# Four weight conversions on ScalarE, each tied behind a copy that TensorE waits for

## The chip, the cores and the metric

The kernel runs on one core of one Trainium2 chip. The metric is the device time of one execution in microseconds (us). TensorE (PE) multiplies, ScalarE (ACT) and VectorE (DVE) copy and do elementwise work, GpSimd (POOL) helps with transposes, and SyncE (SP) issues most transfers.

## The reference, cut to what matters

```python
# q, k, v: (8 batches, 8 heads, 576 tokens, 64), float32
kv = einsum('bhsd,bhse->bhde', k, v)
out = einsum('bhsd,bhde->bhse', q, kv)
rms = sqrt(mean(out * out, axis=-1, keepdims=True) + 1e-06)
x = (out / rms * g_norm)            # then laid out as (4608 tokens, 512)

a = x @ w1                          # w1, w2: 512 x 1024
b = x @ w2
h = a * b @ w3                      # (a * b) @ w3, w3: 1024 x 1024
return h @ w_out                    # w_out: 1024 x 512, result float32
```

The weights w1, w2, w3 and w_out arrive as 64-bit floats, and the kernel turns them into 32-bit floats itself. w3 and w_out are multiplied with each other once ("folded"), so that each group of tokens needs only `(a * b) @ (w3 @ w_out)`. g_norm is multiplied into w1 and w2.

## The kernel before

The tokens are worked on in nine groups of 512. Before the first group there are two halves of eight steps in which w3 and w_out are folded. Each step turns a chunk of w3 on PE, copies the turned chunk from PSUM with ScalarE, and multiplies. Batch 0 of the attention and the conversion of weights run beside it. A conversion handles 128 x 1024 values, in two halves: `begin_next` does two operations on ScalarE, `end_next` four on VectorE and, for w1 and w2, the scaling by g.

```python
def conversion(n, dst, raw, cols=slice(0, 1024), scale=None, by_scalar=False):
    ...
    low = ab[n % 2][:, NF // 2:]...                      # one of two buffers
    nc.scalar.activation(low, lo, AF.Copy, scale=2.0 ** -51, bias=2.0)      # line 157
    nc.scalar.activation(dst, hi.bitcast(FP32), AF.Abs)                     # line 158
    yield                                                # here begin_next ends
    nc.vector.scalar_tensor_tensor(out=low_bits, in0=hi, ...)               # line 160
    nc.vector.tensor_scalar(out=dst, ..., op0=ALU.max, op1=ALU.min)         # line 164
    nc.vector.tensor_scalar(out=dst_bits, ..., op0=ALU.logical_shift_left)  # line 167
    nc.vector.tensor_tensor(out=dst_bits, in0=dst_bits, in1=low_bits, op=ALU.add)   # line 170
    if scale is not None:
        scale_by(dst, scale, by_scalar)   # line 133 on ScalarE in the first group, else line 135 on VectorE

def turn_w3(half, c):
    ...four transposes on PE (line 583)...
    nc.scalar.copy(w3T[half, c], t_ps)                                      # line 588

def fold_chunk(half, c, ms):
    for m in ms:
        nc.tensor.matmul(sums_ps[half][m], lhsT=w3T[half, c][:, m, :], ...) # line 596
        if c == KF - 1:
            nc.scalar.copy(w3o_sb[:, half * NH + m, :], sums_ps[half][m])   # line 601

def turn(r):                                             # x, normed, turned for the products
    ...four transposes on PE (line 449)...
    nc.scalar.copy(dst, t_ps.rearrange("p (i j) t -> p i (j t)", i=2))      # line 451
```

The products with w1 and w2 are done in four blocks p = 0 to 3, each with seven products of half the size in place of eight. PE works on one product (8 matmuls) while ScalarE copies the last one out of PSUM. Copies and products stand in this order; `r1` and `r2` are PSUM banks that are written again, so each copy has to be done before the next product in its bank begins:

```python
def winograd(lhsT, rhs, chunks, done, between=lambda: None):
    ...
    def keep(name, ps):
        ...
        nc.scalar.copy(t, ps)                                               # line 630
    r1 = product("a11", "b11")                                              # line 617, all products
    p1 = keep("p1", r1)
    r2 = product("s1", "t1")
    p5 = keep("p5", r2)
    product("s2", "t2", r1)
    u2 = keep("u2", r1)
    between()                                            # attention of the next batch, in p = 1 to 3
    product("s4", "b22", r2)
    done("c12", r2, u2)
    product("s3", "t3", r1)
    u3 = keep("u3", r1)
    done("c22", p5, u3)
    r3 = product("a12", "b21")
    done("c11", r3, p1)
    between()
    product("a22", "t4", r1)
    done("c21", r1, None)
```

`done` adds and multiplies on VectorE (lines 756, 757, 753) or copies on ScalarE (line 752). The sums s1 to s4 of the weights (lines 670, 671) and the differences t1 to t4 of x (line 660) are made by VectorE. `between` brings in kv products (line 332, copied by line 343), turned q (line 351, copied by line 353) and q times kv (line 415).

The main loop for the first group, T == 0:

```python
for p in range(NF):
    ...
    gates(T, p, between if T or p else lambda: None)     # the seven products of block p
    if T == 0:
        if p + 1 < NF:
            run(sum_w(p + 1))
        for _ in range(2):
            if len(converted) < len(todo):
                begin_next()
                end_next()
```

Four conversions are left for this loop: two at p = 0 (the two halves of the weights for block 2) and two at p = 1 (those for block 3). The order of instructions on PE, GpSimd and SyncE is as written. In this part of the kernel, that on ScalarE and VectorE is chosen by a scheduler when the program is built; it does not know when a transfer lands.

Of the kernel before, what the change touches and what calls it, by code (L numbers as in the profile page):

```python
# [21 lines left out]
def kernel(  # L22
# [32 lines left out]
    nc = tc.nc  # L55
# [26 lines left out]
    def bank(pool, tag):  # L82
        return pool.tile([P, 512], FP32, name=tag, tag=tag)


    loaded = {}
    q_left = {}

    kv_left = [const.tile([P, H, D], FP32, name=f"{name}l_sb") for name in "kv"]
# [129 lines left out]
    def conversions(n):  # L219

        what, i = todo[n]
        if what == "w":
            dst = w_sb[:, i].rearrange("p w c f -> p (w c f)")

            return [conversion(n, dst, raws[n], scale=g_col, by_scalar=in_first_group)]
        if what == "b":
            return [conversion(n, chunks[:, 2 * i:2 * i + 2, 0, :], raws[n])]
        dst = chunks[:, i].rearrange("p w f -> p (w f)")
        cuts = [[0, 256, 512, 1024], [0, 512, 1024], [0, 1024]][min(i, 2)]
        return [conversion(n, dst, raws[n], slice(a, b)) for a, b in zip(cuts, cuts[1:])]  # L230
# [4 lines left out]
    def begin_next():  # L235
        if len(begun) < len(todo):
            begun.append(conversions(len(begun)))
            for c in begun[-1]:
                next(c)
# [25 lines left out]
    xT = {B: x_left}  # L265
# [48 lines left out]
    def attention(b):  # L314
# [129 lines left out]
        def turn(r):  # L444

            t_ps = bank(ps_at, "at").rearrange("p (j t) -> p j t", j=J)
            m = 2 * (r % 2)
            for j in range(J):
                nc.tensor.transpose(t_ps[:, j, :], st[r // 2][:, j // 2, j % 2, m:m + 2, :], ident)  # L449
            dst = xT[b][:, r // 2, :, r % 2, :]  # L450
            nc.scalar.copy(dst, t_ps.rearrange("p (i j) t -> p i (j t)", i=2))

        def x_by_dma(h):

# [63 lines left out]
    def steps(b):  # L518

        a = batch(b)
        a.start()
        more = b + 1 < B
        fs, ends = ([[] for _ in range(8)] for _ in range(2))

        def turn(i, f, *args, next_group=False):

            t = []  # L530

            def begin():
                t.append(f(*args))
                next(t[0])
                next(t[0])

            fs[i].append((begin,))
            (to_end if next_group else ends[i + 1]).append((lambda: all_of(t[0]),))

        if to_end:  # L540

            ends[0] += [(lambda: nc.gpsimd.tensor_copy(tick, late["p5"][:, 0, 0:1]),), *to_end]
        to_end.clear()
        odd = b % 2
        if b == 1:
            fs[0] += [(a.begin_kv, 0, 1), (a.begin_q, 0, 1)]
        fs[1] += [(a.begin_kv, 2, 3), (a.finish, 0)]
        if b == 1:
            fs[2] += [(a.q_t_left,), (a.begin_q, 2, 3)]
            fs[3] += [(a.turn, 0), (a.turn, 1)]  # L550
        else:
            turn(1, a.q_two_by_dma, 2, 3)
            turn(2, a.x_by_dma, 0)
            if odd:
                turn(1, a.q_left_by_dma)
        second = 5 if b == 1 else 4
        if more:
            fs[second].append((batch(b + 1).begin_kv, 0, 1))
        fs[second].append((a.finish, 1))
        if odd:  # L560
            fs[second].append((a.product_left,))
        if b == 1:
            turn(6, a.x_by_dma, 1)
            turn(7, a.x_left_by_dma, next_group=True)
        else:
            turn(5, a.x_by_dma, 1)
            if odd:
                turn(5, a.x_left_by_dma, next_group=more)
        if more:
            turn(7 if b == 1 else 5, batch(b + 1).q_two_by_dma, 0, 1, next_group=True)  # L570
            fs[7 if odd else 0].append((load_q_left, b + 1))
        return iter([lambda s=e + f: [f(*args) for f, *args in s] for e, f in zip(ends, fs)])
# [34 lines left out]
    def late_tile(name):  # L607
        return late_pool.tile([P, 7, P], FP32, name=name[0] if name[0] == "u" else name)

    def winograd(lhsT, rhs, chunks, done, between=lambda: None):  # L610


        def product(a_name, b_name, to=None):
            ps = to if to is not None else bank(ps_mm, "mm").rearrange("p (u n) -> p u n", u=2)
            for u in range(2):
                for c in range(chunks):
                    nc.tensor.matmul(  # L617
                        ps[:, u, :],
                        lhsT=lhsT(a_name, u, c),
                        rhs=rhs(b_name, c),  # L620

                        start=(u == 0 and c == 0 and to is None),
                        stop=(c == chunks - 1),
                        skip_group_check=True,
                    )
            return ps

        def keep(name, ps):
            t = late_tile(name)[:, 0:4, :].rearrange("p (u a) n -> p u (a n)", u=2)
            nc.scalar.copy(t, ps)  # L630
            late[name] = t
            return t

        r1 = product("a11", "b11")
# [16 lines that stand above are left out]
# [78 lines left out]
    def sum_ab(p):  # L729
        aa[p] = {f"a{i + 1}{j + 1}": ab[j][:, p, i, :] for i in range(2) for j in range(2)}  # L730
        return sums(aa[p], free["ab", p])
# [94 lines left out]
    def load_b():  # L826
        n = len(loaded_b)
        if n == ALL_B:
            return
        t = streams[n % len(streams)]  # L830

        part = {ALL_B - 2: 6, ALL_B - 1: 7}.get(n, n % 7)

        queue = nc.scalar if n % 7 in (3, 5) else nc.sync
        if n + 1 < ALL_B:
            queue.dma_start(out=t, in_=w3o_l2[part])
        else:
            t = t[:, 0:1024]
            queue.dma_start(out=t, in_=w3o_l2[part, :, 0:1024])
        loaded_b.append(t)  # L840
# [260 lines left out]
    for n, T in enumerate(groups):  # L1101
        pieces = steps(T + 1) if n + 2 < NG else iter([])

        def between():
            next(pieces, lambda: None)()
            if T == 1:
                for _ in range(2):
                    if next(preparing, 0) == 0 and len(loaded_b) < 3:
                        load_b()

        for p in range(NF):
            if T and p + 1 == NF:
                sum_1, sum_2, sum_4, sum_3 = sum_ab(p)
                following = {
                    "c12": [], "c22": [sum_1],
                    "c11": [
                        lambda: sum_inner(0, lambda: all_of(f() for f in (sum_2, sum_3))),
                        lambda: sum_inner(1),
                    ],
                    "c21": [sum_4],  # L1120
                }

                in_order = tc.manual_schedule(engines={mybir.EngineType.DVE})
                in_order.__enter__()
                gates(T, p, between, lambda name: all_of(f() for f in following[name]))
                continue
            gates(T, p, between if T or p else lambda: None)
            if T == 0:
                if p + 1 < NF:
                    run(sum_w(p + 1))  # L1130
                for _ in range(2):
                    if len(converted) < len(todo):
                        begin_next()
                        end_next()
                if p + 1 == NF:
                    allocate_projection()
                    run(*(f(i) for i in range(NF) for f in (sum_ab, combine_w3o)))
            else:
                run(sum_ab(p))
        last = n + 1 == NG  # L1140
        if T:
            project_twice(T, last, [] if last else combine_x(groups[n + 1]))
            in_order.__exit__(None, None, None)
            continue
        project(T, between)
        run(combine_x(1))
        preparing = prepare_b()
        third = late_pool.tile([P, 3, 2, P], FP32, name="inner_sums")
        inner_sums.append([third[:, i] for i in range(3)])
# [30 lines left out]
```

## Time and profile before

| | |
|---|---|
| time, three runs | 768.45, 769.53, 770.31 us |
| span of the profiled run | 769.8 us |
| busy ScalarE | 252.7 us, 33% |
| busy VectorE | 543.7 us, 71% |
| granted TensorE clock | 1.000 |

The page of a profile gives shares of engines and a chain of waits, followed back from the last instruction. A timeline lists instructions with their start, length, engine, line, operation and tiles, and in brackets the idle time of that engine just before, with what ended it. PEld is TensorE's loading of weights, which overlaps with its matmuls. "w_sb" are the converted w1 and w2, "raw" the 64-bit weights as loaded, "ab" buffers that hold turned w3 or halves of conversions before they hold a * b, "mm" and "at" banks of PSUM, "ws" sums of weights, "xc" and "xT" the x of a group.

### The profile page before, as it was taken

How to read it: one execution, taken by the hardware profiler on the slowest of the kernel's cores; microseconds unless marked ns; L12 is line 12 of the kernel's file. 1: busy time of each engine (PE TensorE's matmuls, PEld its weight loads, DVE VectorE, ACT ScalarE, POOL GpSimd, SP SyncE). 2: the span in 40 equal slices, each digit the busy share in tenths (PEclk: the TensorE clock that was granted, in tenths of full speed). 3: DMA queues.
4: the chain of work that ended last, by engine and by line, in shares of the span. 5: the costliest groups of instructions: out<-in, count | busy, mean ns of one | idle time of the engine just before them, and what ended most of it. 6: DMA issues, size and time to landing. Idle time of an engine off the chain costs nothing.

```text
span 769.8 us, 14414 instructions
## 1 busy us (share of the span) xinstructions
PE 760.1 (99%) x5775; PEld 661.2 (86%) x5775; DVE 543.7 (71%) x1083; ACT 252.7 (33%) x479; POOL 136.2 (18%) x132
## 2 busy tenths in 40 slices
PE   8999999999999999999999999999999999999998
PEld 6455688888899889988998899889988998898897
DVE  7978999548978568856775687557755864495467
ACT  6777744313322332233222321232133222222221
POOL 0000000123520442043114411331144000000000
PEclk9999999999999999999999999999999999999999
DMA  9997532329997834874487448734842370064015
GB/s 324 324 333 213 186 120 60 84 69 267 323 296 265 235 101 115 275 215 102 122 269 206 116 138 267 200 103 132 284 83 50 139 251 1 1 239 152 1 32 195
DMA packets 133159, 132.55 MB, mean 172 GB/s; under 512 B 76644, under 2 KB 121188, under 8 KB 133092
## 3 DMA queue, kind: packets, MB, share of 16 engines
q1 hardware_dynamic: 130640, 116.81, 51.3%
q10 hardware_dynamic: 2452, 14.81, 5.5%
q8 instruction: 46, 0.75, 0.4%
q14 instruction: 21, 0.17, 0.1%
HBM read 100.27 MB, written 16.38 MB: 152 GB/s over the span
## 4 chain that ended last, share of the span: by engine, by line
PE 92%; DMA 5%; SPq 1%; ACT 1%; issue 0%; DVE 0%; ACTq 0%
PE mm L617 60%; PE mm L894 20%; PE mm L596 6%; PE at L332 3%; PE at L415 2%; DMA raw<-w3o_l 2%; DMA raw<-in_moe_w_dram 1%; DMA raw<-in_moe_w_out_dram 1%; DMA w3o_sb<-w3o_l 1%; PE at L583 1%; SPq L95 0%; PE at L945 0%; PE at L351 0%; ACT ab L157 0%; PE at L449 0%
## 5 line engine op out<-in xcount | busy, mean ns | idle before, releaser
L617 PE MATMUL mm<-xT,w_sb 128*128 128x256 f32 x768 | 176.2, 379 | 0.0
L617 PEld LDWEIGHTS mm<-xT,w_sb 128*128 128x128 f32 x768 | 145.6, 190 | 19.8 <-issue 0.5
L617 PE MATMUL mm<-xc,ws 128*128 128x256 f32 x576 | 130.5, 379 | 0.0
L617 PEld LDWEIGHTS mm<-xc,ws 128*128 128x128 f32 x576 | 109.4, 190 | 15.1 <-ACT p L630 0.4
L756 DVE TENSOR_TENSOR c<-mm,u 128x512 f32<-128x512 f32 x36 | 24.8, 690 | 105.5 <-PE mm L617 105.5
L630 ACT COPY u<-mm 128x512 f32<-128x512 f32 x74 | 43.3, 585 | 136.7 <-PE mm L617 125.6
L630 ACT COPY p<-mm 128x512 f32<-128x512 f32 x74 | 43.4, 586 | 86.9 <-PE mm L617 83.4
L617 PE MATMUL mm<-xc,w_sb 128*128 128x256 f32 x288 | 69.0, 382 | 0.0
L290 POOL COPY xT<-xn 128x1024 uint16<-128x1024 uint16 x26 | 31.5, 1240 | 180.1 <-DVE xn L393 180.1
L596 PE MATMUL mm<-chunks,ab 128*128 128x512 f32 x128 | 60.4, 604 | 2.6 <-ACT ab L588 2.6
L894 PE MATMUL mm<-w3o_sb,raw 128*128 128x128 f32 x500 | 62.3, 276 | 0.0
L757 DVE TENSOR_TENSOR ab<-c 128x256 f32<-128x256 f32 x108 | 59.6, 552 | 3.0
L617 PE MATMUL mm<-xT,ws 128*128 128x256 f32 x256 | 61.1, 382 | 0.0
L617 PEld LDWEIGHTS mm<-xc,w_sb 128*128 128x128 f32 x288 | 53.9, 190 | 7.7 <-ACT u L630 0.3
L894 PEld LDWEIGHTS mm<-w3o_sb,raw 128*128 128x128 f32 x500 | 59.0, 192 | 0.2 <-DVE raw L852 0.2
L617 PEld LDWEIGHTS mm<-xT,ws 128*128 128x128 f32 x256 | 48.0, 190 | 6.6
L384 DVE TENSOR_REDUCE inv<-sq 128x8 f32<-128x512 f32 (+1 forms) x40 | 23.4, 627 | 39.4 <-ACT sq L383 39.4
L756 DVE TENSOR_TENSOR c<-p,u 128x512 f32<-128x512 f32 x36 | 27.5, 765 | 25.6 <-ACT u L630 25.5
L894 PE MATMUL mm<-w3o_sb,ab 128*128 128x128 f32 x336 | 44.0, 275 | 0.8 <-DMA w3o_sb<-w3o_l 0.8
L596 PEld LDWEIGHTS mm<-chunks,ab 128*128 128x128 f32 x128 | 21.8, 190 | 25.3 <-issue 15.8
L905 ACT COPY u<-mm 128x512 f32<-128x512 f32 x23 | 13.5, 586 | 87.9 <-DVE raw L918 60.1
L894 PEld LDWEIGHTS mm<-w3o_sb,ab 128*128 128x128 f32 x336 | 41.1, 192 | 1.2 <-issue 0.9
(162 smaller groups left out, 1148.5 us busy)
## 6 DMA issues: line engine op xcount, KB each, us to landing
w3o_sb<-w3o_l SPq DMA_DIRECT2D x26, 896.0 KB, 5.4
raw<-in_moe_w_dram SPq DMA_DIRECT2D x31, 512.0 KB, 7.5
raw<-w3o_l SPq DMA_DIRECT2D x13, 896.0 KB, 5.9
w3o_sb<-w3o_l ACTq DMA_DIRECT2D x11, 896.0 KB, 4.6
k_sb<-in_k_dram SPq DMA_DIRECT2D x32, 256.0 KB, 3.9
v_sb<-in_v_dram SPq DMA_DIRECT2D x32, 256.0 KB, 4.4
q_sb<-in_q_dram SPq DMA_DIRECT2D x32, 256.0 KB, 4.3
out_dram<-raw SPq DMA_DIRECT2D x14, 512.0 KB, 3.5
```

The source lines that it names most:

```text
L290: nc.gpsimd.tensor_copy(to, src.rearrange("p a n w -> p w a n"))
L332: nc.tensor.matmul(kv_ps[e * D:(e + 1) * D, r - rs[0], :], lhsT=k_sb[:, e, cols] if j < J else kl[:, 2 * r + e, :], rhs=v_sb[:, e, cols] i ...
L384: nc.vector.tensor_reduce(out=inv[:, i], in_=sq.rearrange("p (h d) -> p h d", d=D), axis=AX.X, op=ALU.add)
L415: nc.tensor.matmul(o_ps[l][tokens, n * D:(n + 1) * D], lhsT=qT[r][rows, e, i, tokens], rhs=kv_b[rows, e, r, :], start=True, stop=True,)
L583: nc.tensor.transpose(t_ps[:, m, :], src, ident)
L596: nc.tensor.matmul(sums_ps[half][m], lhsT=w3T[half, c][:, m, :], rhs=chunks[:, c, 1, :], start=(c == 0), stop=(c == KF - 1),)
L617: nc.tensor.matmul(ps[:, u, :], lhsT=lhsT(a_name, u, c), rhs=rhs(b_name, c),  start=(u == 0 and c == 0 and to is None), stop=(c == chunks ...
L630: nc.scalar.copy(t, ps)
L756: nc.vector.tensor_add(c, one, two)
L757: nc.vector.tensor_mul(dst, c[:, 0, :], c[:, 1, :])
L894: nc.tensor.matmul(to[:, i, :], lhsT=x[:, c, :], rhs=y[:, c, :], start=new and place // 4 not in seen, stop=(c == 1), skip_group_check=True,)
L905: nc.scalar.copy(t[:, 0:4], ps[0])
```

## The change

Each of the four remaining conversions begins behind a named copy. `issue_after(ins)` adds an ordering edge without a semaphore: the instructions of the block that run on the same engine as `ins` (the two ScalarE operations of `begin_next`) are placed after it in that engine's order. The aim is that a conversion, whose raw weights may not have landed and whose result is needed only one or two blocks later, does not stand in ScalarE's queue before copies that TensorE needs next.

```diff
-    loaded = {}
+    loaded, copies = {}, {}
...
-            nc.scalar.copy(dst, t_ps.rearrange("p (i j) t -> p i (j t)", i=2))
+            copies["xT"] = nc.scalar.copy(dst, t_ps.rearrange("p (i j) t -> p i (j t)", i=2))
...
-            nc.scalar.copy(t, ps)
+            copies.setdefault(name, []).append(nc.scalar.copy(t, ps))
...
-                for _ in range(2):
+                for n in range(2):
                     if len(converted) < len(todo):
-                        begin_next()
+                        ahead = [copies["xT"] if p == 0 else copies["u3"][0], copies["u2"][p]][n]
+                        with tc.issue_after(ahead.ins):
+                            begin_next()
                         end_next()
```

So the four stand behind: the last copy of x; u2 of block 0; u3 of block 0; u2 of block 1. ScalarE's order around the first of them, built from both programs (line, operation, output<-input):

```
before                                 after
L388 inv<-inv                          L388 inv<-inv
L157 ab_75<-raw                        L588 ab_76<-at
L588 ab_76<-at                         L451 xT<-at x2
L158 w_sb<-raw                         L157 ab_75<-raw
L451 xT<-at x2                         L601 w3o_sb<-mm x2
L601 w3o_sb<-mm                        L158 w_sb<-raw
L158 w_sb<-raw                         L601 w3o_sb<-mm x2
L601 w3o_sb<-mm x3                     L630 p1, p5, u2
L158 w_sb<-raw                         L158 w_sb<-raw
L630 p1, p5                            L157 ab_76<-raw
L158 w_sb<-raw                         L133 w_sb<-w_sb
L630 u2                                L630 u3
L133 w_sb<-w_sb                        L157 ab_75<-raw
L157 ab_75<-raw, ab_76<-raw            L158 w_sb<-raw
L630 u3                                L752 c
```

The orders on PE, GpSimd and SyncE do not change. On VectorE the operations are the same and are interleaved otherwise: the four sums of the weights for block 0 (L670, L671) and the first difference of x (L660) now come before the first conversion's L160, and the steps of the conversions shift against the sums and products of blocks 0 to 3.

## The prediction

> **What bounds the kernel now.** I read the page's engine shares first, then the chain that ended last, then the waits of TensorE, and last the order of time around the one wait the change can touch.
>
> ```profile
> PE 760.1 (99%) x5775; PEld 661.2 (86%) x5775; DVE 543.7 (71%) x1083; ACT 252.7 (33%) x479; POOL 136.2 (18%) x132
> ```
>
> TensorE is busy in 760.1 of 769.8 us, so all other engines together can give back at most the 9.7 us in which it is not. The chain of waits puts 92% of the span on PE. Where the rest is, the list of PE's own waits says (engine, line, releaser: us in total, times, longest):
>
> ```profile
> PE mm L596 <- ACT ab L588: 2.6, 2, 1.3
> PE mm L271 <- POOL ident masks.py:199: 1.9, 1, 1.9
> PE mm L894 <- DMA raw<-w3o_l: 0.8, 2, 0.6
> PE mm L894 <- DMA w3o_sb<-w3o_l: 0.8, 1, 0.8
> ```
>
> The reader is to see that PE waits for ScalarE twice only, both times for the copy of the turned w3 chunk (L588), and never for VectorE. One of the two lies at 16.17 us, before anything the change moves. The other is this one. The first lines below are the chain in order of time (start, us, what), the rest the timeline (start, us, engine, line, operation, in brackets the idle time before it and its releaser):
>
> ```profile
> 72.68 8.05 DMA raw<-in_moe_w_dram
> ...
> 80.82 1.12 ACT ab L157
> 81.94 0.49 ACT ab L588
> ...
> 82.47 3.70 PE mm L596 x8
> ```
>
> ```profile
> 78.73 0.60 PE L583 MATMUL at<-ident,chunks 128*128 128x128 f32 x4
> ...
> 80.02 1.18 PE L449 MATMUL at<-ident,xn 128*128 128x128 f32 x8
> 80.08 0.68 DVE L670 TENSOR_TENSOR ws<-w_sb 128x512 f32<-128x512 f32 x1
> 80.21 0.75 PEld L449 LDWEIGHTS at<-ident,xn 128*128 128x128 f32 x7 [0.40 <-DVE xn L393]
> 80.82 1.12 ACT L157 ACTIVATE ab<-raw 128x1024 f32<-128x1024 uint32 x1 [2.34 <-DMA raw<-in_moe_w_dram]
> 81.84 0.58 ACT L588 COPY ab<-at 128x512 f32<-128x512 f32 x1
> 81.97 1.23 DVE L160 SCALAR_TENSOR_TENSOR ab<-raw,ab 128x1024 uint32<-128x1024 uint32 x1 [1.22 <-ACT ab L157]
> 82.31 1.16 ACT L158 ACTIVATE w_sb<-raw 128x1024 f32<-128x1024 f32 x1
> 82.47 0.30 PEld L596 LDWEIGHTS mm<-chunks,ab 128*128 128x128 f32 x2 [1.51 <-ACT ab L588]
> 82.47 3.70 PE L596 MATMUL mm<-chunks,ab 128*128 128x512 f32 x8 [1.27 <-ACT ab L588]
> ```
>
> The turns of the last w3 chunk start at 78.73 and end at 79.33. Their copy L588 could start just after that, but it starts at 81.84, because the first half of a weight conversion (L157) stands ahead of it on ScalarE, and that one stood idle for 2.34 us until its raw weights landed. PE had nothing but the fold that reads this copy and lost 1.27 us. From 82.47 on PE shows no wait until 239.24 us.
>
> **What the Trainium skill says.** "PSUM — Partial Sum Buffer", section "Engine vs sequencer instructions": the queues of ScalarE and VectorE are strictly first in, first out. The trace agrees: L588 had its input for 2.5 us (79.33 to 81.84) and went only after L157. "Perfetto Trace Analysis", section "Optimization Strategy": look for the gaps on the bound engine and what signals their end, then let that start sooner. This change does that to one gap. "Perfetto Trace Analysis", section "Optimizing Scalar/DVE Operations", adds that engines that are not saturated can still cause bubbles elsewhere; at 33% busy ScalarE does so here.
>
> **The change part by part.** No instruction of computation is added or removed. The order of the built program on PE and on the load queue is the same as before, and ScalarE has the same 396 rows in another order. VectorE's operations are the same too, merely interleaved otherwise.
>
> 1. *First conversion, behind the x copies.* On ScalarE the order L157, L588, L158, two copies of x (L451) becomes L588, two L451, L157. Then L588 starts when the turns are done. In the chunk before, the turns started at 73.57 and their copy at 74.26, that is 0.69 later; so here 78.73 + 0.69 = 79.42, ending at about 80.0. PE's eight turns of x run to 81.20, so the fold no longer waits for L588. One detail: in the new program the wait for L588 sits on the second four of the x turns, at about 80.5; 80.0 is before that. Saved: the 1.27 us of the bracket, perhaps 0.1 more, since PE's matmuls otherwise start before the modelled end of the last (80.02 against 79.16 + 1.02 = 80.18). I take 1.3.
>
> 2. *What comes behind it on ScalarE.* The copies of x: the second ended 0.81 us after the end of its turns the time before (64.70 to 65.51), so about 82.0. L157 then runs to 83.1 (its data landed at 80.7), two drains of the fold (L601, about 0.55 each) to 84.1, L158 to 85.2, two drains to 86.3. PE, from 81.2, does the fold to about 84.7 (8 at 0.43), the first product to 86.4 (8 at 0.216 is 1.73), and so on by 1.73. Its copies p1, p5 and u2 are ready to go at about 86.6, 88.3 and 90.1 and find ScalarE free. The bank that the second product needs is drained at 83.6, needed at 86.4.
>
> 3. *Second conversion, behind u2.* L158, L157 and the scaling L133 of the first conversion follow u2: 90.7 + 3 x 1.1 is about 94.0, then u3 to 94.5. The last product of this block overwrites u3's bank and starts at 81.2 + 3.5 + 6 x 1.73 = 95.1. It holds by about half a us. This is the narrowest place I find. L133 waits for VectorE's last step of that conversion (L170): on VectorE the four sums L670 and L671 to 82.8, t1 to 83.4, L160 to 84.6, three combinations to 86.4, then L160, twice L164, twice L167, twice L170 (1.13 + 4 x 0.6 + 2 x 1.13 = 5.8) to 92.2, where L133 wants it at 92.8.
>
> 4. *Third and fourth, behind u3 and the next u2.* Before, all four L158 ran between 82.31 and 91.34. Now those of the third and fourth come after 95 and 102. Their weights are first needed in the sums for the last block, which ran from 116.00 to 121.3 before and are read by PE near 130. The kv and q copies of the next batch move behind one more L158 and stay at about 105 to 107; their reader (L415) is at 112.28 before. Nothing there ends on the path.
>
> 5. *VectorE.* It is busy in 49.90 of the 49.90 us from 82.50 to 132.40, so it must be as early as PE. Its 1.22 us of idle time before L160 (81.97) goes away, as the four sums no longer stand behind L160. So it gains 1.2 where PE gains 1.3.
>
> Sum: -1.3 + 0 + 0 + 0 + 0 = -1.3 us; 769.53 - 1.3 = 768.2 us. It should last to the end, since what later transfers wait for (buffers that PE's products release) moves with PE. From 245 us on each group repeats the same chain.
>
> **Rivals.**
> *A new wait takes the place of the old.* The u3 copy (half a us of room) or a VectorE sum comes late, and PE stops in the blocks between 90 and 130. For it: VectorE has no idle time there, and ScalarE gets conversions right between copies that PE waits for. Against it: in steps 3 and 4 every copy is ahead of its reader by 0.5 us or more, and before, too, u3 (ended 95.62) came 0.75 ahead of the reader at 96.37. It would give back 0.3 to 1.0 us: 768.5 to 769.2. If two or three such stops come together, 770.
>
> *The transfers absorb it.* PE waits for weight parts read back from memory at 239.24 (0.19), 546.76 (0.76) and 689.48 (0.64). If those landings stood at fixed times, a PE that is 1.3 early would wait 1.3 longer at the first, and the time stays at 769.5. Against it: in the chain this transfer starts at 232.52, at the end of PE's products, so it is tied to PE.
>
> *More than the gap.* The freer ScalarE and VectorE could help other waits. But none is left on PE between 82.47 and 239.24, so there is nothing to gain there.
>
> **Range and chances.** The three runs before span 768.45 to 770.31, 1.86 us, more than the whole effect; a median of a few may be off by some 0.6. With 0 to 1.4 us of gain and that scatter, 767.0 to 769.4 should hold it 8 times in 10. 2% would be 15.4 us; PE's idle time in the whole span is 9.7, so faster by 2% cannot be reached. A loss of 15 us would need a stop in each of the blocks, for which I see no cause. So 0.99 for within 2%, 0.003 for faster, 0.007 for slower.
>
> **What would show it.** Right: no idle time before the fold at about 81.1 (the list of PE's waits has L588 once, 1.3 in total), ScalarE's L588 starting at 79.4, its first L157 near 82.0, and PE without waits to 238. Wrong in step 1: L588 still late, or a wait before the second x turns. Wrong in step 3: PE idle for ScalarE's u near 95, or L133 held by L170. Wrong in step 5: PE waiting for ws or xc. Rival two: the idle time at 239 grown to 1.4 us. The prediction fails if the span falls by over 2.5 us or rises.

## The result, and the profile after

The changed kernel took 767.76 us (median of five, 767.41 to 768.26) against 769.59 for the kernel before: a ratio of 0.9975, 95% interval 0.9963 to 0.9987, so 1.8 us less, with 1.0 to 2.8 as the interval. In a second measurement (13 executions, 33 of the kernel before) the ratio was 0.9987 (0.9978 to 0.9996), 1.0 us less.

PE's waits in the changed kernel (engine, line, releaser: us in total, times, longest):

```profile
PE mm L271 <- POOL ident masks.py:199: 2.0, 1, 2.0
PE mm L596 <- ACT ab L588: 0.7, 1, 0.7
PE mm L596 <- ACT chunks L158: 0.6, 1, 0.6
```

L588 stands there once in place of twice, with a wait of 0.66 us at 15.62, at the start of the kernel. The waits of L894 for transfers are gone too, in this profile; the experiments show that this is no work of the change. The timeline of the changed kernel where the gap was (start, us, engine, line, operation, idle time before):

```profile
78.20 0.60 PE L583 MATMUL at<-ident,chunks 128*128 128x128 f32 x4
...
78.83 0.59 ACT L588 COPY ab<-at 128x512 f32<-128x512 f32 x1 [0.88 <-PE at L583]
...
79.50 1.18 PE L449 MATMUL at<-ident,xn 128*128 128x128 f32 x8
...
80.27 1.07 ACT L451 COPY xT<-at 128x512 f32<-128x512 f32 x2 [0.85 <-PE at L449]
...
80.51 3.60 PE L596 MATMUL mm<-chunks,ab 128*128 128x512 f32 x8
...
81.23 1.19 ACT L157 ACTIVATE ab<-raw 128x1024 f32<-128x1024 uint32 x1
```

L588 now waits for its own turns only, is done at 79.42, and the fold follows the turns of x at 80.51 without idle time. L157 comes after the copies of x and finds its data landed: it has no wait of its own.

Executions differ by more than the effect. In the profiles below the last turns begin anywhere between 77.6 and 79.8 us, and the part from line 894 to the end takes 544.9 to 547.0. So I compare the stretch the change alters: from the start of the last turns of w3 (the last L583) to the first product of the projection (L894), by the starts of matmuls in each timeline. "Block 0" is from the first product to the first L332; "block 1" from there to the turn of the left q (L368), which includes most of block 2's first half.

| kernel | turns to first product | block 0 | block 1 | whole stretch |
|---|---|---|---|---|
| before | 7.28 | 17.36 | 17.20 | 144.13 |
| before, again | 7.49 | 17.36 | 17.20 | 144.42 |
| changed | 5.74 | 17.36 | 16.95 | 142.34 |
| changed, again | 5.75 | 17.35 | 16.94 | 142.33 |
| first tied alone | 5.74 | 18.09 | 16.94 | 143.37 |
| last three tied | 6.67 | 17.36 | 16.94 | 143.26 |
| first and fourth tied | 5.74 | 17.57 | 16.94 | 142.54 |
| first behind the w3 copy | 5.74 | 17.36 | 16.94 | 142.53 |
| loaded early, no ties | 6.65 | 17.79 | 16.94 | 143.67 |
| u3 copied four times | 5.74 | 18.65 | 17.07 | 143.75 |

Both profiles of the changed kernel agree to 0.01 us. Against the two of before the change is worth 1.8 and 2.1 us: 1.54 and 1.74 before the first product, 0.25 in block 1. That second part is one more wait for ScalarE, which the prediction had not seen. In the kernel before, PE's weight loads show it (the load is held until the copy p has emptied the bank):

```profile
118.73 1.38 PEld L617 LDWEIGHTS mm<-xc,ws 128*128 128x128 f32 x7 [0.39 <-ACT p L630]
```

ScalarE in the kernel before, and then in the changed kernel, up to that copy:

```profile
114.77 1.15 ACT L133 ACTIVATE w_sb<-w_sb,g_col 128x1024 f32<-128x1024 f32 x1 [1.37 <-DVE w_sb L170]
115.94 1.08 ACT L383 ACTIVATE sq<-at 128x512 f32<-128x512 f32 x2
116.92 0.38 ACT L752 COPY c<-mm 128x256 f32<-128x256 f32 x1
117.90 0.31 ACT L388 ACTIVATE inv<-inv,eps_col 128x16 f32<-128x16 f32 x1 [0.61 <-DVE inv L384]
118.12 1.25 ACT L630 COPY p<-mm 128x512 f32<-128x512 f32 x2
```

```profile
111.36 1.08 ACT L383 ACTIVATE sq<-at 128x512 f32<-128x512 f32 x2
113.45 1.15 ACT L133 ACTIVATE w_sb<-w_sb,g_col 128x1024 f32<-128x1024 f32 x1 [1.01 <-DVE w_sb L170]
115.31 0.31 ACT L388 ACTIVATE inv<-inv,eps_col 128x16 f32<-128x16 f32 x1 [0.71 <-DVE inv L384]
115.52 0.35 ACT L752 COPY c<-mm 128x256 f32<-128x256 f32 x1
115.78 0.59 ACT L630 COPY p<-mm 128x512 f32<-128x512 f32 x1
```

Before, the scaling L133, which waits for VectorE, stood ahead of the squares L383 and so ahead of the norm's L388 and the copy p1 of block 2. After, L383 goes first, VectorE's sums of squares lie beside the wait, and p1 starts 2.3 us earlier in the profile, of which 2.1 is the shift PE has anyway (its last product of block 1 begins at 113.30 before and 111.23 after). One profile below has the old order back: in "u3 copied four times" L133 (114.89) stands ahead of L383 (116.06) again, and block 1 takes 17.07 in place of 16.94.

### The profile page after: what moved, and what is told of

Read it like the earlier page. It is cut to its first block, busy times and chain, and to the rows that moved or that the text cites. A ratio compares the mean times of both kernels' runs of the same rounds, so it can differ in the third digit from the quotient of the medians.

```text
span 765.4 us, 14413 instructions
## 1 busy us (share of the span) xinstructions
PE 758.5 (99%) x5775; PEld 660.1 (86%) x5775; DVE 543.9 (71%) x1083; ACT 253.3 (33%) x479; POOL 136.6 (18%) x132
## 4 chain that ended last, share of the span: by engine, by line
PE 97%; DMA 1%; ACT 0%; issue 0%; SPq 0%; DVE 0%; ACTq 0%
PE mm L617 60%; PE mm L894 23%; PE mm L596 7%; PE at L332 3%; PE at L415 2%; DMA raw<-in_moe_w_out_dram 1%; PE at L583 1%; PE at L351 1%; PE at L945 0%; DMA raw<-in_moe_w_dram 0%; PE at L449 0%; PE at L434 0%; ACT ab L157 0%; ACT chunks L158 0%; ACT kv_sb L343 0%; PE mm L434 0%
## 5 line engine op out<-in xcount | busy, mean ns | idle before, releaser
L756 DVE TENSOR_TENSOR c<-mm,u 128x512 f32<-128x512 f32 x36 | 24.8, 689 | 103.3 <-PE mm L617 103.3
L894 PE MATMUL mm<-w3o_sb,raw 128*128 128x128 f32 x500 | 62.4, 276 | 0.0
L894 PEld LDWEIGHTS mm<-w3o_sb,raw 128*128 128x128 f32 x500 | 59.0, 192 | 0.4 <-DVE raw L852 0.2
L756 DVE TENSOR_TENSOR c<-p,u 128x512 f32<-128x512 f32 x36 | 26.5, 736 | 27.5 <-ACT u L630 27.4
L894 PE MATMUL mm<-w3o_sb,ab 128*128 128x128 f32 x336 | 43.7, 275 | 0.0
L894 PEld LDWEIGHTS mm<-w3o_sb,ab 128*128 128x128 f32 x336 | 41.0, 192 | 0.3
```

The costliest lines, as they stand in the source:

```text
L756: nc.vector.tensor_add(c, one, two)
L894: nc.tensor.matmul(to[:, i, :], lhsT=x[:, c, :], rhs=y[:, c, :], start=new and place // 4 not in seen, stop=(c == 1), skip_group_check=True,)
```

## The experiments

**First tied alone.** Edit against the changed kernel:

```diff
-                        with tc.issue_after(ahead.ins):
+                        with tc.issue_after(ahead.ins) if (p, n) == (0, 0) else ExitStack():
```

> Only the first conversion is tied (behind the copies of x); the other three are left to the scheduler. Theory A (the gain is the head of ScalarE's queue at the last w3 chunk): no idle time before the last fold, L588 about 0.7 us after its turns begin, and nearly the whole gain, -1.4 to -1.8 us against the kernel before. Theory B (the later ties do half of it by freeing ScalarE for the copies p and u): -0.7 us or less. Theory C (the gain is scatter of transfers read back from memory at lines 894): no relation to the tie, the products before 200 us end where they ended before.

Measured: ratio 0.9993 (0.9985 to 1.0002), 0.5 us less, not clear of noise. The gap before the fold is closed as in the changed kernel (5.74 us to the first product), but block 0 takes 0.73 us longer. ScalarE in block 0 of this kernel:

```profile
86.19 1.24 ACT L158 ACTIVATE w_sb<-raw 128x1024 f32<-128x1024 f32 x1
87.25 0.66 ACT L630 COPY p<-mm 128x512 f32<-128x512 f32 x1
89.04 1.16 ACT L158 ACTIVATE w_sb<-raw 128x1024 f32<-128x1024 f32 x1 [1.14 <-DMA raw<-in_moe_w_dram]
90.10 0.58 ACT L630 COPY u<-mm 128x512 f32<-128x512 f32 x1
```

The fourth conversion's L158 stands before u2 and waits 1.14 us for its raw weights. u2 could have been copied at about 88.8; it ends at 90.68, and the next product in its bank starts late. So Theory A as I put it falls short: the first tie closes the gap, but PE, once earlier, runs into the next conversion whose weights are late. In the kernel before, that L158 started at 90.15 without a wait.

Why these weights are late, the chain of the same profile shows (start, us, what):

```profile
82.80 1.07 ACT w_sb L158
...
83.89 0.37 SPq L195
...
84.31 4.65 DMA raw<-in_moe_w_dram
```

Their load (L195) does not start at a fixed time. SyncE issues it 0.02 to 0.03 us after the end of the first conversion's L158, in nine of the ten profiles (all but "loaded early"). The first tie puts the copies of x and two drains of the fold ahead of that L158, so the load goes out 6.26 us after the last turns begin, in place of 4.77 and 5.00 in the two profiles of before. This delay of 1.3 to 1.5 us is as large as the wait of 1.14; that it accounts for all of the wait is an estimate, since the transfers themselves took 5.07 us here and 5.95 before. So the tie that brings PE forward also pushes the fourth load back, and the later ties make up for it.

The rest of this kernel's loss against the changed one (0.3 us) arises at 197.57 us, where PE's weight load waits 0.41 us for a copy p, and p for VectorE. VectorE is late because an addition (L756) at 192.09 took 1.69 us in place of 0.69: it started 0.01 us after a GpSimd copy. In the changed kernel's profile that addition started 0.45 us before the copy and took 0.69. In a profile of before it took 1.52 with no such wait behind it, so this part depends on how the engines happen to meet.

**Last three tied.** The same line with `(p, n) != (0, 0)`.

> The last three conversions are tied, the first is not. Theory A: the wait of 1.27 us before the last fold is still there (L588 behind L157, which waits for its raw weights), and the time is that of the kernel before to within 0.3 us. Theory B: -0.7 us or more without the gap being closed.

Measured: ratio 0.9998 (0.9988 to 1.0009). The gap is still there:

```profile
79.61 1.17 ACT L157 ACTIVATE ab<-raw 128x1024 f32<-128x1024 uint32 x1 [1.68 <-DMA raw<-in_moe_w_dram]
80.67 0.59 ACT L588 COPY ab<-at 128x512 f32<-128x512 f32 x1
...
81.31 3.70 PE L596 MATMUL mm<-chunks,ab 128*128 128x512 f32 x8 [0.66 <-ACT ab L588]
```

In this execution the raw weights landed earlier, and the gap is 0.66 us. With the two profiles of before this gives three points: L157 starts 1.43, 2.09 and 2.31 us after the turns begin, and the first product comes 0.93, 1.54 and 1.75 us later than in the changed kernel. From the first to the third L157 is 0.88 us later and PE 0.82: nearly all of the lateness is lost. So the gain of the change depends on the execution, and the tie makes PE independent of it: in the six profiles with the first conversion tied these weights landed between 0.1 and 2.0 us after the turns began (1.4, 2.0 and 2.2 in the three just named), and the first product always comes after 5.74 or 5.75 us. The block 1 part (16.94) is gained here without the first tie.

**Loaded early, no ties.** Edit against the kernel before:

```diff
-        FIRST = len(converted) + KF - 1
+        FIRST = len(converted) + KF
```

> The kernel before without any tie, but the raw weights of the first of the four conversions are loaded one step earlier, ahead of the k, v and q of the next batch. Theory A in its second half (what cost the time is the late landing, not the work of L157): the gap closes as well, -1.3 to -1.8 us, with no wait of L157 for a transfer. If the work of L157 itself (1.1 us) were the cost, at least half of the gap would stay: -0.7 us or less.

Measured: ratio 1.0037 (1.0022 to 1.0051), 2.8 us slower, the opposite of what I expected. In the program that the scheduler built, the conversion stands earlier too:

```profile
70.32 1.14 ACT L158 ACTIVATE w_sb<-raw 128x1024 f32<-128x1024 f32 x1 [0.73 <-DMA raw<-in_moe_w_dram]
71.36 0.57 ACT L588 COPY ab<-at 128x512 f32<-128x512 f32 x1
...
71.98 2.84 PE L596 MATMUL mm<-chunks,ab 128*128 128x512 f32 x6 [1.86 <-ACT ab L588]
```

The same gap, two chunks earlier and larger: 1.86 us. Behind the last turns PE also waits for VectorE's normed x (L393), 0.43 and 0.20 us, so the first product comes after 6.65 us although L588 is in time there. The run does not tell the lateness of the landing from the work of L157, as it was meant to, since both moved. It does show that an earlier load alone is no cure here: the order still puts a conversion before a copy that PE waits for.

**u3 copied four times.** The changed kernel with three more copies before u3 of block 0:

```diff
+            if name == "u3" and name not in copies:
+                for _ in range(3):
+                    nc.scalar.copy(t, ps)
             copies.setdefault(name, []).append(nc.scalar.copy(t, ps))
```

> The changed kernel with the copy u3 of block 0 made four times in place of once (the same values): 3 x 0.49 = 1.46 us more on ScalarE just where the prediction saw the narrowest place. In the trace of the changed kernel u3 ends at 93.58 and its reader starts at about 94.3, so 0.7 us of room: PE should stop for 0.7 to 0.8 us before the last product of block 0, and the time be 0.75 us above that of the changed kernel, about 1.1 us under the kernel before. If the room is larger than it looks (over 1.5 us), nothing is lost; if there is none, 1.5 us is lost.

Measured: ratio 1.0014 (1.0005 to 1.0024), 1.1 us over the kernel before. ScalarE, and then PE (L632 and L633 are the copies here, since lines were added):

```profile
92.95 1.14 ACT L133 ACTIVATE w_sb<-w_sb,g_col 128x1024 f32<-128x1024 f32 x1
94.02 1.82 ACT L632 COPY u<-mm 128x512 f32<-128x512 f32 x3
95.88 0.59 ACT L633 COPY u<-mm 128x512 f32<-128x512 f32 x1
```

```profile
91.88 3.62 PE L617 MATMUL mm<-xT,w_sb 128*128 128x256 f32 x16
96.52 1.99 PE L617 MATMUL mm<-xc,w_sb 128*128 128x256 f32 x8 [1.02 <-ACT u L633]
```

The extra copies cost 95.88 - 94.02 = 1.86 us, more than the 1.46 I had put. The last product of block 0 was due at 91.88 + 3.45 = 95.33 and starts at 96.52, 1.19 late; after this wait its eight matmuls take 0.10 more, so block 0 grew by 18.65 - 17.36 = 1.29. The room before u3 in the changed kernel is then 1.86 - 1.19 = 0.67 us. The changed kernel's own profile gives the same: u3 ends at 93.58 and its reader starts at 94.30, and a product that does wait starts 0.05 after its copy ends (96.47 to 96.52 here). So what exceeds the room is lost in full.

The time misses my expectation by 2.2 us: the stretch is 1.4 us over the changed kernel's and still 0.4 to 0.7 under that of before, but the time is 1.1 over. In its profile the last turns begin at 79.23 us, after a wait of 2.0 us in the folding at the start; the profile of "first and fourth tied" has the same wait (1.9 us), so it is no mark of this kernel. Where its 13 executions lost the time was not found; it stays open.

**The changed and the kernel before once more.**

> The changed kernel once more, on the same chip and against the same runs as those below. From the start of the last turns of w3 to the first product of the projection (line 894) the profile before has 144.1 us, after 142.3, tied first alone 143.4. If that stretch is what the change alters, it is 142.3 again (to 0.2) and the time is 1.4 to 1.9 us under the kernel before; the waits of lines 894 for transfers (2.1 us in the profile of before, none in that of after) come and go by themselves, here too.

> The kernel before once more, for a second profile of it. The stretch from the last turns to line 894 should be 143.5 to 144.2 us (the raw weights land a little earlier or later from run to run), with L588 behind L157; the waits of lines 894 for transfers need not be where they were, which would show them to be scatter.

Measured: the changed kernel at 0.9987 (0.9978 to 0.9996), its stretch 142.33; the kernel before has 144.42, 0.2 over the range I expected, since the weights landed later still (L157 2.31 us after the turns). The time gains 1.0 us, under my 1.4 to 1.9, whose lower end is within the interval (0.3 to 1.7). The waits for transfers come and go as expected, in the kernel before and then in the changed one:

```profile
PE mm L596 <- ACT ab L588: 2.3, 2, 1.5
PE mm L271 <- POOL ident masks.py:199: 2.0, 1, 2.0
PE mm L596 <- DVE chunks L170: 1.0, 1, 1.0
PE mm L894 <- DMA raw<-w3o_l: 0.4, 1, 0.4
```

```profile
PE mm L271 <- POOL ident masks.py:199: 2.0, 1, 2.0
PE mm L596 <- DVE chunks L170: 1.4, 1, 1.4
PE mm L596 <- ACT ab L588: 1.0, 1, 1.0
PE mm L894 <- DMA w3o_sb<-w3o_l: 0.6, 1, 0.6
```

The waits of L894 for transfers are scatter in both kernels, and so are those of the first folds. The difference of the first two spans, 4.4 us, therefore overstates the change by more than two: 0.5 of it lies ahead of the turns and 2.1 behind line 894. The changed kernel's second profile has 545.7 us from line 894 to the end, the same as the second of before.

**First and fourth tied.** The same line with `(p, n) in ((0, 0), (1, 1))`.

> The first and the fourth conversion are tied, the second and the third are not. With the first tied alone, block 0 took 18.09 us in place of 17.36, because the fourth conversion's L158 stood before u2 and waited for its raw weights until 89.0. If that one wait is what the later ties guard against, block 0 is 17.4 us here and the whole stretch from the last turns to line 894 is 142.3 to 142.6, as with all four. If the work of the conversions between p1, p5 and u2 costs it, over 17.7.

Measured: ratio 0.9995 (0.9985 to 1.0006); block 0 17.57, 0.2 over the 17.4 I expected; whole stretch 142.54, as expected. Of the 0.73 us that block 0 lost with the first tie alone, the fourth tie takes back 0.52, the wait for the late weights. The other 0.21 lies here:

```profile
92.28 1.15 ACT L133 ACTIVATE w_sb<-w_sb,g_col 128x1024 f32<-128x1024 f32 x1
93.33 1.15 ACT L157 ACTIVATE ab<-raw 128x1024 f32<-128x1024 uint32 x1
94.39 0.56 ACT L630 COPY u<-mm 128x512 f32<-128x512 f32 x1
```

The third conversion's L157 stands before u3. u3 ends at 94.95, and the product that reads its bank was due at 84.54 + 6 x 1.727 = 94.90. It starts at 95.00 and takes 0.10 more after the wait. Ahead of this, the second conversion's L157 had waited 0.63 us for VectorE (at 91.14). So the second and third ties together are worth these 0.2 us; no run leaves out one of them alone.

**First tied behind the w3 copy.** Edits against the changed kernel:

```diff
-        nc.scalar.copy(w3T[half, c], t_ps)
+        copies["w3T"] = nc.scalar.copy(w3T[half, c], t_ps)
...
-                        ahead = [copies["xT"] if p == 0 else copies["u3"][0], copies["u2"][p]][n]
+                        ahead = [copies["w3T"] if p == 0 else copies["u3"][0], copies["u2"][p]][n]
```

> The first conversion is tied behind the copy of the turned w3 (L588) in place of the copies of x; the other three as in the change. If only L588 has to be ahead of it, nothing is lost: first product 5.7 us after the last turns begin, stretch to line 894 142.3 us, time as the changed kernel's. If the copies of x have to be ahead too, VectorE's differences of x come late and PE waits 0.5 us or more in block 0.

Measured: ratio 0.9995 (0.9985 to 1.0005), median 768.52 against 768.57 of the changed kernel in the same set. Its first product comes after 5.74 us and block 0 takes 17.36; the whole stretch is 0.2 longer, all of it at 211.91, where PE's weight load waits 0.33 us for a copy p. VectorE is late there, after standing idle for 2.79 us (at 207.32) until a GpSimd copy (L304), which had itself waited for a transfer. So only L588 has to be ahead of the first conversion. In this execution the weights had landed when L157 started at 79.41; with a late landing the copies of x would wait for it, which this run does not test. Here the first L158 is early again, and the load of the fourth conversion goes out 4.50 us after the turns. So this tie alone, without the other three, might do; no run tries it.

No run shows a kernel faster than the changed one: from the last turns to line 894 no matmul of PE stands in the list of its waits. Two waits of its weight loads are left there, 0.40 us for xn at 79.68 and 0.22 for kv_sb at 140.35; both were there before, and what they cost was not tried.

## Why the prediction was right, and where it was not

The prediction put 768.2 us and 767.0 to 769.4; measured was 767.76, and the mechanism of the main term is the predicted one. The time alone does not show the size: the two measurements gave 1.8 us (1.0 to 2.8) and 1.0 (0.3 to 1.7), and both agree with 1.3. The stretch says 1.8 to 2.1, so the agreement with -1.3 is partly luck.

One sign of being wrong that I had named came true: the span of the profiled executions fell by 4.4 us, over the 2.5 I had set. The sign was badly chosen. Two profiles of the same kernel before differ by 1.5 us (769.8 and 768.3), and 2.6 of the 4.4 lie outside the stretch that the change alters.

- *Step 1* (-1.3): right in mechanism, too small by 0.2 to 0.4. L588 started 0.63 us after the turns (predicted 0.69), the fold 2.31 (predicted 2.4), and the first product comes 1.54 us earlier against the profile the prediction read, 1.74 against the second. The bracket of 1.27 is counted from the modelled end of the turns of x. Undisturbed, the fold starts 0.17 before that end (80.51 against 79.50 + 1.18), and after a wait its eight matmuls take 0.11 more to the first product (86.01 - 82.47 = 3.54 against 83.94 - 80.51 = 3.43). 1.27 + 0.17 + 0.11 = 1.55. I had allowed 0.1 for that and rounded it away. For the same reason PE's 9.7 us of idle time, which I took as the most that can be won, is no strict bound.
- *Step 2* (0): right. Before p1, p5 and u2 of block 0 ScalarE waits for PE only, and block 0 takes 17.36 us as before.
- *Step 3* (0, "about half a us" of room): right. Four copies of u3 showed 0.67.
- *Step 4* (0, "Nothing there ends on the path"): wrong by one term. Between blocks 1 and 2 there was a wait of PE's weight load for p1 (0.39 in PEld), which the list of PE's own matmul waits does not show because a matmul's modelled end covered it. The new order removes it: -0.25. With it the sum is -1.8 to -2.0, as the stretch shows.
- *Step 5* (VectorE keeps up): right. VectorE is busy 47.82 of the 48.00 us from 82 to 130 in the changed kernel, and in its one idle moment there (0.18, at 108.92) it waits for u3.
- *Rivals.* The first, a new wait in the place of the old, does not occur with all four ties, but it is what the first tie alone runs into. The second, absorbed by transfers at fixed times, is not seen at line 894: the part behind it was no longer in the changed kernel than before. Something like it holds for the raw weights of the fourth conversion, though not because they land at a fixed time: their load waits for the first conversion's L158, which the change itself moves back. The later ties are the answer to it. That is the piece of the mechanism I had not seen: I took steps 3 and 4 as things to survive, whereas they protect 0.7 us of step 1. The third, more than the gap, I ruled out because PE had no other wait in the list of its matmuls; the 0.25 in block 1 is just that, seen on the weight load.

## What to carry to other kernels

On an in-order engine that feeds the bound engine, an operation which waits for a transfer belongs behind the copies that the bound engine needs next, not where the program first has room for it. When such an operation is moved back, look at what its end sets free: here the next load started behind it, and so landed later against an engine that came earlier. Look also at the waits of the weight loads, not only of the matmuls. For an effect of a fifth of a per cent compare the length of the stretch that changes in a profile; whole times still left 1.4 us of interval with 13 executions against 33.

## What the runs showed of the hardware

The start of the same transfer's consumer moved by 0.9 us between executions (1.43 to 2.31 us after the same point of the program), and PE's loss moved with it. Three copies of the same 128x512 tile into the same place started 0.62 us apart each (1.86 for three), where a copy and the independent operation after it are 0.48 to 0.49 apart (89.32 to 89.80, 92.99 to 93.48 in the changed kernel). A GpSimd copy can hold up a VectorE addition. In the ten profiles, 62 of the additions of L756 whose operands are both in SBUF (c<-p,u) began with 0.16 us or more of a GpSimd copy still to come. Each ended 0.54 to 0.55 us after that copy did, and they took 0.74 to 1.69 us; 254 such additions without a GpSimd copy took 0.68 to 0.69. 163 additions with one operand in PSUM (c<-mm,u and c<-mm,p) began in the same way, and took 0.68 to 0.69 all the same.
